# A third addition of u and of its square, and one of e, ahead of the sums of chunks 1 to 4, with another order of the work

## The chip, the cores and the metric

The kernel runs on one core of a Trainium2 chip. The metric is the device time of one execution in microseconds. The core has five engines, each of which works through its own list of instructions in order: PE (matmuls; a weight load goes ahead of each), DVE and ACT (elementwise work), POOL (elementwise work, and the issue of most loads) and SP (which here only issues transfers).

## What is computed

Linear attention without a softmax, normalized by head, is followed by a feed-forward layer with SoLU (h times the softmax of h) and a layer norm inside. In the reference, for 8 batches of 8 heads with 576 rows of 64, and a feed-forward of 512 to 1024 to 512 on all 4608 rows:

```python
kv = np.einsum('bhsd,bhse->bhde', k, v)
out = np.einsum('bhsd,bhde->bhse', q, kv)
rms = np.sqrt(np.mean(out * out, axis=-1, keepdims=True) + 1e-06)
x = out / rms * g_norm            # heads side by side: 4608 x 512
h = x @ w_in
e = np.exp(h - h_max)
solu = h * (e / (np.sum(e, axis=-1, keepdims=True) + 1e-09))
ln = (solu - mu) / np.sqrt(var + 1e-06) * g_ln
return ln @ w_out
```

## The kernel before

The rows go in nine **chunks** of 512: chunks 0 to 7 take eight of every nine rows of one batch each, and chunk 8 takes the ninth row of all batches. The names below are those of the kernel's table of work; the first number is the chunk or batch.

- `kv_mm` multiplies k by v of a batch on PE, and `kv` casts the products out of PSUM. Batches 0 and 1 come in two halves of four heads (second number 0 and 1); `qT_mm` and `qT` turn q. `o_mm` gives o, `sq` squares it on ACT, `oa` adds the two halves of the squares, and `s_mm` sums them by head. `ex` (chunk 0: one instruction; later `ln` and `ex`) gives the reciprocal root, and `x` (L489, DVE) scales o by it. `table` loads ACT's second function table between the two kinds of root.
- `h` (L532) multiplies x by w_in: eight blocks per chunk, four matmuls each, in two parts for chunks 0 to 2. `exp` (L539, ACT) makes e, and `u` (L543, DVE) is h times e. `usq` (L233 on ACT or L235 on POOL) is u squared, and `es` (L551, POOL) adds e of two neighbouring blocks, so that eight become four.
- The layer norm needs three sums over all 1024 columns, of u, u squared and e. **`sums`** (L594) makes them on PE, as matmuls with a small selecting matrix, four for each block of 512 that is left. Before that, `ua`, `usqa` and `esa` (all L575, in `fold`, on DVE) add the upper half of the blocks to the lower half: `FOLDS` says how often for u and u squared (eight blocks become four, two, one) and `E_FOLDS` for e (four become two). `turn` (L601), `stats` and `rstd` make the factor of each row of it.
- `w_mean` and `w_center` prepare w_out once, with the mean and the weight of the layer norm in it. `out` (L651) multiplies u by it, four blocks of rows per chunk, eight matmuls each; the last block of chunk 8 is done in two halves of columns (L659). `ob` (L239 on ACT, L241 on DVE) scales by `rstd`, and `store` sends it off.
- `warm` (L300) is matmuls on zeros whose result nobody reads; `WARM` holds how many there are at each of seven places. `ident` (POOL) makes the identity for `qT_mm`, and `wide` loads the second half of k and v of batch 0 as float32 through SP, which `k.0.1` and `v.0.1` cast.

Nothing here is scheduled by a compiler. `ORDER` is a table of all the pieces of work, written out by hand or by a program, and `Plan.emit` records them one by one: each engine's list is what the table gives it in this order, with the engine behind a colon where it isn't the usual one. `ROOMS` holds a digit for each tile that says which of its slots it takes; for the tiles in PSUM that is one of eight banks, and a piece that takes a bank waits until the work on what stood there is done. So an instruction waits for its data, for its room, and for all that stands ahead of it on its engine. Beyond that, `Plan.run` makes each POOL instruction wait for the additions that DVE was given ahead of it:

```python
if engine == "pool":
    self.after(ins, self.adds)
    self.adds.clear()
if name[0] in ("ua", "usqa", "esa", "oa") and engine == "dve":
    self.adds.append(ins)
```

Of the kernel before, what the change touches and what calls it, by code (L numbers as in the profile page):

```python
# [25 lines left out]
kv.1.0.0.0 kv.1.0.1.1 kv.1.0.1.0 qT_mm.1.0 ex.0.0 q.2.0 qT.1.0:act x.0.0.0 x.0.0.1 warm.5 o_mm.1.0 sq.1.0.0 warm.6
h.0.6.0 h.0.3.0 k.2.0 sq.1.0.1 x.0.1.0 table h.0.0.0 oa.1.0 x.0.1.1 s_mm.1.0 h.0.2.0 h.0.7.0 h.0.2.1 ln.1.0 v.2.0
ex.1.0 h.0.6.1 x.1.0.1 exp.0.6 q.3.0 h.0.3.1 exp.0.2 x.1.0.0 h.0.7.1 h.0.1.0 exp.0.7 u.0.6 v.3.0 qT_mm.1.1 h.0.0.1
exp.0.3 h.0.1.1 u.0.2 usq.0.6 h.1.2.0 exp.0.0 qT.1.1 kv_mm.1.1.1 exp.0.1 kv_mm.1.1.0 k.3.0 kv.1.1.0.1 h.0.4.0 h.0.4.1
u.0.1 kv.1.1.2.1:act kv.1.1.0.0:act es.0.0 kv.1.1.1.0:act kv.1.1.2.0:act kv.1.1.1.1 u.0.3 o_mm.1.1 exp.0.4 h.0.5.0  # L30
u.0.7 sq.1.1.0 es.0.3 h.0.5.1 u.0.4 sq.1.1.1 h.1.0.0 w_mean.0 usq.0.1:act oa.1.1 u.0.0 exp.0.5 s_mm.1.1 ln.1.1 ex.1.1
u.0.5 es.0.2 w_mean.1 w_mean.2 w_mean.3 w_mean.4 w_mean.5 w_mean.6 usq.0.5:act x.1.1.1 usq.0.2 usq.0.7:act w_mean.7
x.1.1.0 usq.0.0 q.4.0 usq.0.4:act w_center.5 h.1.3.0 qT_mm.2.1 h.1.7.0 w_center.1 h.1.4.0 h.1.7.1 qT.2.1:act q.5.0
w_center.4 h.1.0.1 v.4.0 w_center.0 exp.1.7 qT_mm.2.0 exp.1.0 w_center.3 h.1.1.0 h.1.1.1 k.4.0 qT.2.0:act w_center.2
h.1.2.1 es.0.1 u.1.7 h.1.3.1 exp.1.1 h.1.4.1 u.1.0 exp.1.3 out.0.2.0 es.1.0 usq.0.3 u.1.1 exp.1.2 out.0.2.1 kv_mm.2.0
w_center.7 exp.1.4 h.1.5.0 w_center.6 kv.2.1.0:act kv.2.0.0:act h.1.5.1 kv.2.0.2:act kv.2.1.1 kv.2.0.1:act es.1.1
u.1.4 out.0.2.2 kv.2.1.2:act exp.1.5 o_mm.2.0 u.1.3 o_mm.2.1 sq.2.0.1 out.0.2.3 usq.1.1 u.1.2 qT_mm.3.0 sq.2.0.0 u.1.5
out.0.0.0 sq.2.1.1 oa.2.0 out.0.0.1 sq.2.1.0 qT.3.0 s_mm.2.0 usq.1.5 out.0.0.2 ln.2.0 qT_mm.3.1 oa.2.1:pool ex.2.0
h.1.6.0 qT.3.1 out.0.0.3 usq.1.2:act x.2.0.0 x.2.0.1 h.1.6.1 s_mm.2.1 exp.1.6 sums.0 usq.1.7 ln.2.1 u.1.6 ex.2.1
kv_mm.3.0 es.1.2 turn.0 stats.0 out.0.3.0 kv.3.1.0:act x.2.1.0 x.2.1.1 usq.1.0:act out.0.3.1 usq.1.4 usq.1.3 h.2.6.0  # L40
out.0.3.2 rstd.0 h.2.0.0 ob.0.0:act usq.1.6 kv.3.0.1 ob.0.2 h.2.6.1 kv.3.1.2:act kv.3.0.0:act kv.3.1.1:act out.0.3.3
usqa.1.0 kv.3.0.2:act h.2.4.0 exp.2.6 h.2.5.0 ob.0.3:act ua.1.0 o_mm.3.0 h.2.1.0 store.0.3 sq.3.0.0 h.2.0.1 sq.3.0.1
u.2.6 h.2.1.1 store.0.0 exp.2.0 h.2.5.1 usqa.1.1 out.0.1.0 exp.2.1 oa.3.0 h.2.4.1 ua.1.1 exp.2.5 qT.4 s_mm.3.0
out.0.1.1 u.2.0 ln.3.0 es.1.3 out.0.1.2 u.2.5 h.2.7.0 ex.3.0 h.2.7.1 u.2.1 exp.2.4 es.2.0 h.2.3.0 x.3.0.1 exp.2.7
o_mm.3.1 sq.3.1.0 x.3.0.0 usq.2.6 out.0.1.3 sq.3.1.1 h.2.2.0 h.2.3.1 u.2.7 qT.5 ob.0.1:act h.2.2.1 oa.3.1 sums.1
exp.2.3 u.2.4 es.2.3 kv_mm.4.0 exp.2.2 u.2.3 store.0.1 usq.2.5:act s_mm.3.1 turn.1 es.2.2 out.1.3.0 kv.4.1.0
kv.4.0.1:act ln.3.1 u.2.2 store.0.2 out.1.3.1 kv.4.0.0 usq.2.7 ex.3.1 stats.1 out.1.2.0 kv.4.0.2:act kv.4.1.1 kv.4.1.2
rstd.1 x.3.1.1 usq.2.0 o_mm.4.0 o_mm.4.1 ob.1.3 sq.4.0.1 out.1.0.0 usq.2.4 x.3.1.0 sq.4.0.0 store.1.3 out.1.2.1
sq.4.1.0 oa.4.0 ua.2.0 sq.4.1.1 s_mm.4.0 out.1.0.1 ln.4.0 oa.4.1 h.3.2.0 ex.4.0 ob.1.0 v.5.0 s_mm.4.1 x.4.0.0 h.3.7.0
k.5.0 ln.4.1 x.4.0.1 exp.3.2 es.2.1 h.3.3.0 ex.4.1 u.3.2 h.3.6.0 exp.3.3 ua.2.1 exp.3.7 h.3.5.0 x.4.1.0 u.3.3 v.6.0  # L50
exp.3.6 x.4.1.1 h.3.1.0 exp.3.5 q.6.0 usq.2.2:act h.3.4.0 usq.3.3 ob.1.2:act usq.2.1:act usq.2.3:act exp.3.4 es.3.1
u.3.7 u.3.5 store.1.2 h.4.6.0 u.3.6 k.6.0 u.3.4 h.4.7.0 exp.3.1 out.1.1.0 out.1.1.1 exp.4.7 usq.3.2:act h.3.0.0
usqa.2.0 usqa.2.1 exp.4.6 ob.1.1:act u.4.7 kv_mm.5.0 usq.3.5 exp.3.0 u.3.1 sums.2 kv.5.0.1:act es.3.3 h.4.5.0
usq.4.7:act u.4.6 kv.5.0.0:act kv.5.1.2:act h.4.4.0 q.7.0 kv.5.0.2 kv.5.1.1:act u.3.0 kv.5.1.0:act exp.4.5 o_mm.5.1
es.3.0 turn.2 o_mm.5.0 sq.5.1.0 out.2.3.0 stats.2 u.4.5 sq.5.1.1 out.2.3.1 exp.4.4 oa.5.1 ua.3.0 rstd.2 s_mm.5.1
out.2.0.0 ln.5.1 u.4.4 sq.5.0.0 out.2.0.1 sq.5.0.1 ua.3.1 h.4.0.0 ob.2.3:act oa.5.0 ob.2.0 ex.5.1 s_mm.5.0 es.4.2
store.2.3 h.4.2.0 ln.5.0 x.5.1.0 h.4.3.0 store.1.1 usq.3.6 exp.4.2 x.5.1.1 ex.5.0 usq.3.4:act kv_mm.6.0 u.4.2 usq.3.0
qT.6 out.2.1.0 out.2.2.0 kv.6.1.0 kv.6.0.0 es.4.3 kv.6.1.2 x.5.0.0 out.2.2.1 usq.3.7:act qT.7 x.5.0.1 exp.4.3
usq.3.1:act h.4.1.0 es.3.2 kv.6.1.1:act u.4.3 usq.4.5:act kv.6.0.1 ob.2.2:act store.1.0 usqa.3.0 h.5.3.0 exp.4.1
kv.6.0.2:act h.5.6.0 store.2.0 exp.5.3 exp.4.0 usqa.3.1 u.4.1 h.5.7.0 es.4.0 es.4.1 usq.4.6:act u.4.0 out.2.1.1  # L60
exp.5.6 u.5.3 exp.5.7 o_mm.6.0 ob.2.1 o_mm.6.1 sq.6.0.0 sums.3 u.5.6 store.2.1 out.3.0.0 sq.6.0.1 u.5.7 usq.4.2:act
oa.6.0 out.3.0.1 sq.6.1.1 ua.4.0 sq.6.1.0 s_mm.6.0 out.3.3.0 ln.6.0 oa.6.1 turn.3 out.3.3.1 ex.6.0 v.7.0 stats.3
q_last.3 s_mm.6.1 x.6.0.0 h.5.0.0 ln.6.1 k.7.0 x.6.0.1 h.5.2.0 ex.6.1 q_last.1 exp.5.0 x.6.1.0 h.5.5.0 q_last.7
exp.5.2 u.5.0 h.5.4.0 rstd.3 es.5.1 x.6.1.1 usq.4.4:act out.3.1.0 ob.3.0 exp.5.4 es.5.3 h.6.6.0 usq.4.3:act ob.3.3
usq.4.0:act u.5.4 h.6.3.0 exp.5.5 ua.4.1 h.5.1.0 usq.4.1:act u.5.5 q_last.0 exp.6.6 out.3.1.1 u.5.2 q_last.4
# [670 lines left out]
```

## Time and profile before

| what | value |
|---|---|
| time, median of 3 runs | 177.52 us (177.48 to 177.98) |
| span of the profiled execution | 175.8 us |
| granted clock of TensorE, mean | 1.000 |
| PE / DVE / ACT / POOL busy | 164.2 / 145.5 / 152.1 / 99.8 us |
| matmuls of h and of out in the profile | 280 of 68.0 us, 266 of 65.2 us |
| HBM read, written | 32.51 MB, 9.44 MB |

The span runs from the first to the last instruction in one profiled execution. The times of the runs hold what lies around the span as well; the profiled execution's own time is not given apart from it. Matmuls overlap, so a mean of 379 ns says how long one is under way, not how far apart two start. In the rows, "out<-in" names the tiles written and read, a figure in square brackets or behind the last bar is the idle time of the engine just before, and the name behind an arrow is what ended it.

### The profile page before, as it was taken

The page shows a single profiled execution, that of the slowest core. Times are in us where ns is not written, and L with a number is a line of the kernel's source. Part 1 is how long each engine was busy: PE and PEld are TensorE (multiplying, and loading weights), DVE is VectorE, ACT ScalarE, POOL GpSimd, SP SyncE. Part 2 cuts the span into 40 slices and gives each one's busy share as a digit, 9 for nine tenths or more (in the row PEclk, how much of TensorE's full clock was granted, in tenths as well). Part 3 has the DMA queues.
Part 4 walks back from the last instruction along what each step waited for, and adds up shares of the span by engine and source line. Part 5 has one row for each costly group of instructions (what it writes and reads, how often), then busy time and mean ns, then how long its engine had stood idle before and what let it go on. Part 6 is the DMA issues. An engine that isn't in the chain of part 4 may idle for free.

```text
span 175.8 us, 4843 instructions
## 1 busy us (share of the span) xinstructions
PE 164.2 (93%) x1913; PEld 80.3 (46%) x1938; DVE 145.5 (83%) x317; ACT 152.1 (86%) x273; POOL 99.8 (57%) x108
## 2 busy tenths in 40 slices
PE   7767998798999999999999999999999999999992
PEld 2344344454564354445454444445464444444451
DVE  2015769899899999989999999979997999998732
ACT  2549899998999998999999999999999989999450
POOL 8744359899790794877294567593191257335000
PEclk9999999999999999999999999999999999999999
DMA  5999999999999995899989639983994055024874
GB/s 179 218 203 214 206 275 373 209 208 208 208 210 210 218 210 129 127 206 235 205 183 259 150 52 193 156 73 93 195 206 105 5 118 126 2 60 93 196 213 159
DMA packets 34623, 30.27 MB, mean 172 GB/s; under 512 B 16288, under 2 KB 28328, under 8 KB 34600
## 3 DMA queue, kind: packets, MB, share of 16 engines
...
HBM read 32.51 MB, written 9.44 MB: 239 GB/s over the span
## 4 chain that ended last, share of the span: by engine, by line
PE 75%; DVE 10%; ACT 5%; DMA 5%; issue 2%; POOL 1%; POOLq 0%; DVEq 0%; ACTq 0%
PE h_ps L532 31%; PE out_ps L651 30%; DMA k_sb<-in_k_dram 5%; PE kv_ps L375 4%; PE o_ps L448 3%; DVE u_sb L543 3%; PE sum_ps L594 3%; PE s_ps L465 3%; DVE x_sb L489 2%; DVE w_out_sb L638 2%; ACT osq_sb L233 2%; DVE osq_sb L460 1%; PE out_ps L659 1%; ACT e_sb L539 1%; ACT kvd L229 1%
## 5 line engine op out<-in xcount | busy, mean ns | idle before, releaser
L532 PE MATMUL h_ps<-x_sb,w_in_sb 128*128 128x512 bf16 x280 | 68.0, 379 | 0.5
L651 PE MATMUL out_ps<-w_out_sb,u_sb 128*128 128x512 bf16 x266 | 65.2, 379 | 0.7 <-issue 0.3
L551 POOL TENSOR_TENSOR es_sb<-e_sb 128x512 bf16<-128x512 f32 x36 | 45.4, 1279 | 33.5 <-ACT e_sb L539 13.0
L539 ACT ACTIVATE e_sb<-h_ps,zero_t 128x512 f32<-128x512 f32 x72 | 46.2, 690 | 2.3 <-PE h_ps L532 1.7
L543 DVE TENSOR_TENSOR u_sb<-h_ps,e_sb 128x512 bf16<-128x512 f32 x72 | 46.6, 684 | 1.3 <-ACT e_sb L539 1.0
L532 PEld LDWEIGHTS <-w_in_sb 128*128 128x128 bf16 x288 | 27.3, 98 | 32.5 <-issue 1.3
L651 PEld LDWEIGHTS <-u_sb 128*128 128x128 bf16 x280 | 26.4, 98 | 31.6 <-issue 1.0
L233 ACT ACTIVATE usq_sb<-u_sb,zero_t 128x512 bf16<-128x512 bf16 x49 | 33.6, 718 | 0.0
L489 DVE SCALAR_TENSOR_TENSOR x_sb<-o_ps,g_sb,rst_sb 128x256 bf16<-128x256 f32 x72 | 30.2, 478 | 3.1 <-ACT rst_sb L476 2.5
L235 POOL TENSOR_TENSOR usq_sb<-u_sb 128x512 bf16<-128x512 bf16 x23 | 23.6, 1043 | 7.9 <-DVE osq_sb L460 5.6
L233 ACT ACTIVATE osq_sb<-o_ps,zero_t 128x512 bf16<-128x512 f32 x36 | 22.8, 689 | 3.5 <-PE o_ps L448 3.4
L239 ACT ACTIVATE ob_sb<-out_ps,rstd 128x512 f32<-128x512 f32 x22 | 14.8, 684 | 4.0 <-PE out_ps L651 3.8
L575 DVE TENSOR_TENSOR usq_sb<-usq_sb 128x2048 bf16<-128x2048 bf16 (+2 forms) x20 | 17.0, 848 | 0.6 <-ACT usq_sb L233 0.4
L229 DVE CAST kvd<-kv_ps 64x128 bf16<-64x128 f32 (+3 forms) x26 | 6.4, 256 | 11.2 <-ACT kvd L229 6.5
L241 DVE TENSOR_SCALAR ob_sb<-out_ps,rstd 128x512 f32<-128x512 f32 (+1 forms) x15 | 10.6, 711 | 4.1 <-PE out_ps L659 2.2
L322 POOL DMA_DIRECT2D v_sb<-in_v_dram x9 | 6.8, 757 | 10.1 <-DVE sum_ps L601 2.8
L472 ACT ACTIVATE lss_sb<-s_ps,eps_t 128x512 f32<-128x512 f32 x16 | 11.1, 695 | 1.0 <-PE s_ps L465 0.7
L476 ACT ACTIVATE rst_sb<-lss_sb,zero_t 128x512 f32<-128x512 f32 x16 | 11.5, 722 | 0.4
L375 PE MATMUL kv_ps<-v_sb,k_sb 64*64 64x64 bf16 x576 | 8.0, 194 | 2.8 <-DMA k_sb<-in_k_dram 1.3
L300 PE MATMUL warm_ps<-zeros 128*128 128x512 bf16 x25 | 8.8, 481 | 1.4 <-DVE zeros L255 1.2
L229 ACT CAST kvd<-kv_ps 64x128 bf16<-64x128 f32 (+3 forms) x34 | 8.2, 243 | 2.2 <-PE kv_ps L375 1.5
L375 PEld LDWEIGHTS <-k_sb 64*64 64x64 bf16 x576 | 6.8, 107 | 6.8 <-DMA k_sb<-in_k_dram 2.6
...
## 6 DMA issues: line engine op xcount, KB each, us to landing
...
```

The lines of the kernel that those rows point to most:

```text
L229: nc.scalar.copy(dst, src) if engine == "act" else on[engine].tensor_copy(dst, src)
L233: nc.scalar.activation(out=dst, in_=src, func=AF.Square, bias=zero_t[:, :])
L235: on[engine].tensor_tensor(out=dst, in0=src, in1=src, op=MUL)
L239: nc.scalar.activation(out=dst, in_=src, func=AF.Copy, scale=by)
L375: nc.tensor.matmul(t[64 * y:64 * y + 64, :], T["k", b][rows, n, i, :], T["v", b][rows, n, i, :], start=(i == 0 and (b < 2 or m == 0)), sto ...
L489: nc.vector.scalar_tensor_tensor(out=t[:, 2 * hf + dh, z], in0=T["o", c, hf, z][:, dh], scalar=g_rep[dh], in1=T["rst", c, hf][:, z], op0=M ...
L532: nc.tensor.matmul(bank(("h", c, f), [128, 512])[:, :], w_in_sb[:, dt, f * 128:(f + 1) * 128], T["x", c][:, dt].rearrange("p a b c -> p (a ...
L539: nc.scalar.activation(out=t[:, f % 2, :], in_=T["h", c, f][:, :], func=AF.Exp, bias=zero_t[:, :])
L543: nc.vector.tensor_tensor(out=t[:, f, :], in0=T["h", c, f][:, :], in1=T["e", c, f // 2][:, f % 2, :], op=MUL)
L551: on[engine].tensor_tensor(out=t[:, n, :], in0=e[:, 0, :], in1=e[:, 1, :], op=ADD)
L575: nc.vector.tensor_tensor(out=to[:, 0:n, :], in0=src[:, 0:n, :], in1=src[:, n:2 * n, :], op=ADD)
L651: nc.tensor.matmul(bank(("out", c, m), [128, d_model])[:, :], T["u", c][:, f, m * 128:(m + 1) * 128], w_out_sb[:, f, :], start=(f == 0), s ...
```

## The change

Chunks 1 to 4 get what chunks 5 to 8 had: a third addition of u and of u squared, which leaves one block of each instead of two, and one addition of the e blocks, which leaves two instead of four. So `sums` of these chunks has 4 x (1 + 1 + 2) = 16 matmuls instead of 32. The whole table is another one too: order, engines and rooms differ from the first piece on, and the numbers of matmuls on zeros. The loads through POOL come in the same succession, and the stores nearly so. Counted over the table, these change engines or number:

| pieces | before | after |
|---|---|---|
| additions `ua`, `usqa`, `esa` on DVE | 20, 20, 4 | 24, 24, 8 |
| `oa` on DVE, POOL | 15, 1 | 11, 5 |
| `ob` on DVE (of them halves), ACT (halves) | 15 (2), 22 | 11 (0), 26 (2) |
| `kv` on DVE, ACT | 26, 34 | 21, 39 |
| `usq` on POOL, ACT | 23, 49 | 27, 45 |
| cast of the wide k | ACT | DVE |
| matmuls on zeros | 27 | 42 |

```diff
@@ ORDER, the first and the last lines @@
-wide.v ident wide.k g_rows q.0.1 v.0.0 k.0.0 q.0.0 v.0.1:act v.1.0 k.1.0 q.1.0 w_in.0 k.0.1:act w_in.1 warm.0
-kv_mm.0.1.0 qT_mm.0.1 kv.0.1.0.0:act kv.0.1.1.0 kv_mm.0.1.1 q.1.1 qT.0.1:act kv.0.1.2.1 kv.0.1.2.0 kv.0.1.1.1
...
-out.8.1.1 out.8.3.0 rstd.8 ob.8.2:act ob.8.0 store.8.2:act store.8.0 ob.8.1:act store.8.1:act ob.8.3.0 store.8.3.0
-out.8.3.1 ob.8.3.1 store.8.3.1:act
+wide.v v.0.1:act wide.k g_rows q.0.1 v.0.0 k.0.0 q.0.0 v.1.0 k.1.0 q.1.0 w_in.0 k.0.1 ident warm.0 qT_mm.0.1 w_in.1
+q.1.1 warm.1 kv_mm.0.0.0 kv.0.0.2.0:act kv.0.0.1.0:act kv_mm.0.0.1 v.1.1 k.1.1 w_out.0 w_out.1 kv.0.0.0.1:act
...
+store.8.2 store.8.0:act store.8.1:act ob.8.3.0:act ob.8.3.1:act store.8.3.0 store.8.3.1:act
@@ ROOMS @@
...
@@ WARM @@
-14 3 1 3 1 4 1
+21 11 5 1 1 2 1
@@ tile_transnormer_attn__then__act_solu_kernel @@
-    FOLDS = (0, 2, 2, 2, 2, 3, 3, 3, 3)
-    E_FOLDS = (0, 0, 0, 0, 0, 1, 1, 1, 1)
+    FOLDS = (0, 3, 3, 3, 3, 3, 3, 3, 3)
+    E_FOLDS = (0, 1, 1, 1, 1, 1, 1, 1, 1)
```

Three places, by what stands there on an engine. First ACT in the head, from the squares of o of batch 0 to the table load. Before (`o_ps_303` and `_305` are half 1 of batch 0, `_347` and `_349` half 0, `_458` and `_460` batch 1; `rst_sb` are the reciprocal roots):

```order
L233 ACTIVATE osq_sb_322<-o_ps_303,zero_t_81 128x2x256
L233 ACTIVATE osq_sb_371<-o_ps_347,zero_t_81 128x2x256
L233 ACTIVATE osq_sb_371<-o_ps_349,zero_t_81 128x2x256
L482 ACTIVATE rst_sb_403<-s_ps_373,eps_t_79 128x512
L229 CAST kvd_1_0_0_1_110<-kv_ps_382 128x64
L482 ACTIVATE rst_sb_442<-s_ps_425,eps_t_79 128x512
L229 COPY qT_sb_446<-qt_ps_433 128x1024
L233 ACTIVATE osq_sb_476<-o_ps_458,zero_t_81 128x2x256
L233 ACTIVATE osq_sb_476<-o_ps_460,zero_t_81 128x2x256
L494 ACT_TABLE_LOAD
```

After (here `o_ps_347` and `_349` are half 0, `_422` and `_424` half 1, `_478` and `_480` batch 1):

```order
L233 ACTIVATE osq_sb_391<-o_ps_347,zero_t_81 128x2x256
L233 ACTIVATE osq_sb_391<-o_ps_349,zero_t_81 128x2x256
L482 ACTIVATE rst_sb_397<-s_ps_394,eps_t_79 128x512
L233 ACTIVATE osq_sb_451<-o_ps_422,zero_t_81 128x2x256
L233 ACTIVATE osq_sb_451<-o_ps_424,zero_t_81 128x2x256
L229 CAST kvd_1_0_2_0_113<-kv_ps_371 64x64
L229 CAST kvd_1_0_0_0_109<-kv_ps_371 128x64
L229 CAST kvd_1_0_1_0_111<-kv_ps_371 64x64
L482 ACTIVATE rst_sb_472<-s_ps_467,eps_t_79 128x512
L233 ACTIVATE osq_sb_496<-o_ps_480,zero_t_81 128x2x256
L233 ACTIVATE osq_sb_496<-o_ps_478,zero_t_81 128x2x256
L494 ACT_TABLE_LOAD
```

Half 0 now comes first, with its root; the squares of half 1, three casts for batch 1 and the root of half 1 stand between it and batch 1's squares. The turning copy has gone to DVE.

Second, DVE between chunk 1 and chunk 2. Before, from the scaling of a block of chunk 0 (`ob_sb`) through the additions of chunk 1 (`usq_sb_897`, `ua_sb_1178`) among the first u of chunk 2 (`u_sb_1208`):

```order
L241 TENSOR_SCALAR ob_sb_1157<-out_ps_752,rstd_1148 128x512
L575 TENSOR_TENSOR usq_sb_897<-usq_sb_897 128x2048
L575 TENSOR_TENSOR ua_sb_1178<-u_sb_742 128x2048
L543 TENSOR_TENSOR u_sb_1208<-h_ps_1141,e_sb_1171 128x512
L575 TENSOR_TENSOR usq_sb_897<-usq_sb_897 128x1024
L460 TENSOR_TENSOR osq_sb_1203<-osq_sb_1203 128x512
L575 TENSOR_TENSOR ua_sb_1178<-ua_sb_1178 128x1024
L543 TENSOR_TENSOR u_sb_1208<-h_ps_1150,e_sb_1214 128x512
L543 TENSOR_TENSOR u_sb_1208<-h_ps_1173,e_sb_1227 128x512
```

After, from the last product x of chunk 2 through the additions of chunk 1 (`usq_sb_784`, `ua_sb_1034`, `es_sb_776`) to the first u of chunk 2 (`u_sb_1230`):

```order
L489 SCALAR_TENSOR_TENSOR x_sb_1080<-o_ps_985,g_sb_73,rst_sb_1085 128x256 x2
L229 CAST kvd_3_1_1_131<-kv_ps_1097 64x128
L229 COPY qT_sb_1092<-qt_ps_1175 128x1024
L575 TENSOR_TENSOR usq_sb_784<-usq_sb_784 128x2048
L575 TENSOR_TENSOR usq_sb_784<-usq_sb_784 128x1024
L575 TENSOR_TENSOR ua_sb_1034<-ua_sb_1034 128x512
L575 TENSOR_TENSOR es_sb_776<-es_sb_776 128x1024
L575 TENSOR_TENSOR usq_sb_784<-usq_sb_784 128x512
L543 TENSOR_TENSOR u_sb_1230<-h_ps_1216,e_sb_1228 128x512
L543 TENSOR_TENSOR u_sb_1230<-h_ps_1235,e_sb_1228 128x512
```

The additions of chunk 1 that are left at this place, five of its seven, now stand together ahead of all u of chunk 2; two of u (with 2048 and 1024 elements) stand further up, ahead of that chunk's x.

Third, the end of ACT's list. Before (`out_ps_3197` and `_3272` are blocks of chunk 8):

```order
L615 ACTIVATE lv_3290<-vare_3264,zero_t_81 128x4
L617 ACTIVATE rstd_3292<-lv_3290,zero_t_81 128x4
L239 ACTIVATE ob_sb_3294<-out_ps_3197,rstd_3292 128x512
L675 DMA out_0_dram<-ob_sb_3294 128x512
L239 ACTIVATE ob_sb_3300<-out_ps_3272,rstd_3292 128x512
L675 DMA out_0_dram<-ob_sb_3300 128x512
L675 DMA out_0_dram<-ob_sb_3303 128x256
```

After (`out_ps_3158` and `_3255` are the two halves of the last block):

```order
L615 ACTIVATE lv_3247<-vare_3245,zero_t_81 128x4
L617 ACTIVATE rstd_3249<-lv_3247,zero_t_81 128x4
L239 ACTIVATE ob_sb_3270<-out_ps_3230,rstd_3249 128x512
L675 DMA out_0_dram<-ob_sb_3264 128x512
L675 DMA out_0_dram<-ob_sb_3270 128x512
L239 ACTIVATE ob_sb_3275<-out_ps_3158,rstd_3249 128x256
L239 ACTIVATE ob_sb_3275<-out_ps_3255,rstd_3249 128x256
L675 DMA out_0_dram<-ob_sb_3275 128x256
```

The two last halves, which DVE scaled, now stand on ACT behind the issue of two stores.

More of the change, by code (lines that the diff above doesn't have):

```diff
@@ L26 @@
[L26 to L65, printed above, removed]
@@ new lines @@
+u.8.1 out.6.0.0 out.7.2.0 h.8.2.0 out.7.0.0 out.6.0.1 out.6.1.0 out.6.1.1 u.8.0 u.7.7 h.8.3.0 out.7.0.1 out.6.2.0
+usq.8.0:act ob.6.3 out.6.2.1 out.7.3.0 store.6.3 usq.7.7:act usq.7.0:act usq.7.6:act usq.8.4:act usq.8.7:act es.8.3
+es.8.0 es.7.3 ua.7.0 esa.7.0 exp.8.2 exp.8.3 ua.7.1 ob.6.1:act ob.6.0:act usqa.7.0 usqa.7.1 ua.7.2 usqa.7.2 u.8.3
+sums.7 out.7.3.1 es.8.1 u.8.2 out.8.2.0 store.6.0 usq.8.6:act turn.7 stats.7 es.8.2 esa.8.0 usq.8.1:act out.7.2.1
+out.7.1.0 out.8.3.0 out.7.1.1 ua.8.0 ob.6.2:act out.8.0.0 out.8.0.1 usq.8.2:act rstd.7 ob.7.3:act ob.7.0:act
```

94 lines of the change are left out of this document (65 added, 29 removed).

## The prediction

> **What bounds the kernel now.** I read the page first: the busy times, and the span in 40 equal slices.
>
> ```profile
> span 175.8 us, 4843 instructions
> PE 164.2 (93%) x1913; PEld 80.3 (46%) x1938; DVE 145.5 (83%) x317; ACT 152.1 (86%) x273; POOL 99.8 (57%) x108
> PE   7767998798999999999999999999999999999992
> DVE  2015769899899999989999999979997999998732
> ```
>
> The PE row is full from about the tenth slice to the last but one. There the program is a queue of matmuls, and its time is the start of that queue, plus its matmuls, plus its stops, plus the tail behind it. Next the table of windows, which gives busy us per stretch (columns: span, length, PE, PEld, DVE, ACT, POOL, clock, DMA share, GB/s).
>
> ```profile
> 0.00:5.00 5.00, 3.81 (x9) 1.34 (x10) 0.90 (x14) 1.35 (x2) 4.29 (x13) 1.00 0.59 207
> 5.00:10.00 5.00, 3.57 (x52) 1.84 (x51) 0.80 (x4) 3.52 (x5) 2.92 (x5) 1.00 1.14 191
> 35.00:40.00 5.00, 4.84 (x28) 2.27 (x27) 5.00 (x9) 4.66 (x8) 4.82 (x6) 1.00 1.22 208
> 40.00:45.00 5.00, 4.48 (x123) 2.68 (x126) 4.94 (x10) 4.22 (x11) 3.69 (x5) 1.00 1.22 208
> 45.00:65.00 20.00, 19.82 (x363) 10.15 (x366) 18.81 (x45) 19.23 (x36) 14.22 (x13) 1.00 1.21 207
> 65.00:100.00 35.00, 34.63 (x438) 16.52 (x443) 33.39 (x66) 33.98 (x65) 22.03 (x22) 1.00 0.97 191
> ```
>
> Three stages follow. Before 20 us the input transfers and a chain of short steps set the pace. From there to 45 us DVE has no free time and PE still stops. From 45 us PE is the bound, with little room behind it: DVE has 1.19 us free in 45 to 65 and 1.61 in 65 to 100, ACT 0.77 and 1.02. POOL alone has room.
>
> **The change part by part: the sums.** In the chain of waits, which keeps what PE was held by, sums of a chunk with two additions and of one with three stand side by side:
>
> ```profile
> 119.44 0.56 PE sum_ps L594 x32
> 130.04 0.34 PE sum_ps L594 x16
> ```
>
> Four chunks go from 32 matmuls to 16: 4 x 0.22 = 0.88 us off PE, nearly all where PE is the bound. **Term: -0.9.**
>
> **The additions, and what leaves DVE for them.** From the groups that keep shapes apart:
>
> ```profile
> L575 DVE TENSOR_TENSOR usq_sb<-usq_sb 128x512 bf16<-128x512 bf16 x4 | 1.7, 423 | 0.0
> L575 DVE TENSOR_TENSOR ua_sb<-ua_sb 128x512 bf16<-128x512 bf16 x4 | 1.7, 419 | 0.0
> L575 DVE TENSOR_TENSOR es_sb<-es_sb 128x1024 bf16<-128x1024 bf16 x4 | 2.7, 685 | 0.0
> L460 DVE TENSOR_TENSOR osq_sb<-osq_sb 128x512 bf16<-128x512 bf16 x15 | 6.7, 445 | 1.0 <-ACT osq_sb L233 0.6
> L241 DVE TENSOR_SCALAR ob_sb<-out_ps,rstd 128x512 f32<-128x512 f32 x13 | 9.6, 747 | 1.9 <-ACT rstd L617 1.0 <-PE out_ps L651 0.9
> L229 DVE CAST kvd<-kv_ps 64x128 bf16<-64x128 f32 x10 | 2.9, 289 | 1.5 <-PE kv_ps L375 0.9 <-ACT kvd L229 0.3
> L460 POOL TENSOR_TENSOR osq_sb<-osq_sb 128x512 bf16<-128x512 bf16 x1 | 1.1, 1150 | 0.0
> L235 POOL TENSOR_TENSOR usq_sb<-u_sb 128x512 bf16<-128x512 bf16 x23 | 23.6, 1043 | 7.9 <-DVE osq_sb L460 5.6 <-DVE usq_sb L575 2.2
> L239 ACT ACTIVATE ob_sb<-out_ps,rstd 128x512 f32<-128x512 f32 x22 | 14.8, 684 | 4.0 <-PE out_ps L651 3.8
> L233 ACT ACTIVATE usq_sb<-u_sb,zero_t 128x512 bf16<-128x512 bf16 x49 | 33.6, 718 | 0.0
> ```
>
> Added to DVE: 4 x (0.419 + 0.423 + 0.685) = 6.1 us. Off DVE over the whole program: four additions of o squared (1.8), two full scalings and the last two halves (2.5), five casts (about 1.3); the net is near zero. ACT gets those casts and scalings and loses four squares of u (2.9); POOL gets four squares and four additions of o squared, 4 x (1.043 + 1.150) = 8.8 us, of the 76 it has free. The relief is not where the load is, though. All 6.1 us fall on chunks 1 to 4, that is on 45 to about 110 us; of the relief there, DVE scales five blocks of chunks 0 to 3 where it scaled eight (2.2), adds net two fewer o squares (0.9) and casts two fewer (0.6). That leaves +2.4 us, against the 2.8 us that DVE has free between 45 and 100. So the cost for PE lies between 0 (every free moment gets used) and 2.4 (none does). The order shows the worst place: behind the last product x of chunk 2, five additions of chunk 1 now stand in one row, about 3.4 us by their rows, ahead of the first u of chunk 2, and PE's later products of chunk 2 need the banks that u frees. Before, two additions stood ahead of it. I take 1.0, below the middle, since the rest is spread out. **Term: +1.0.**
>
> A rule weighs against this part. The additions have two operands in SBUF; one of them met a POOL instruction:
>
> ```profile
> 30.23 0.79 DVE L460 TENSOR_TENSOR osq_sb<-osq_sb 128x512 bf16<-128x512 bf16 x1
> 28.21 2.52 POOL L551 TENSOR_TENSOR es_sb<-e_sb 128x512 bf16<-128x512 f32 x2
> ```
>
> It took 0.79 us instead of 0.445 and ended 0.3 us after POOL did, at 30.73. The Trainium skill, "SBUF — State Buffer", section "Who interferes with whom", says that such a DVE instruction and a POOL instruction that reads SBUF exclude each other, and the later one waits for the whole of the earlier. The trace agrees at this place. By that rule alone, with each of twelve additions waiting half of a 1.28 us POOL addition, the sum would be 7.7 us more; by the rows, it is next to nothing, since hardly any addition of the program is longer than its group's mean, the kernel making each POOL instruction wait for the additions ahead of it.
>
> **The head.** The order of the two halves of batch 0 is turned round. Rows of the timeline (start, length):
>
> ```profile
> 14.08 0.62 PE L448 MATMUL o_ps<-qT_sb,kvd 64*32 64x256 bf16 x16 [0.29 <-ACT kvd L229]
> 15.77 0.76 PE L375 MATMUL kv_ps<-v_sb,k_sb 64*64 64x64 bf16 x36
> 19.11 0.43 PE L448 MATMUL o_ps<-qT_sb,kvd 64*32 64x256 bf16 x16 [0.24 <-DVE x_sb L489]
> 19.84 1.47 PE L532 MATMUL h_ps<-x_sb,w_in_sb 128*128 128x512 bf16 x6
> 14.28 1.84 ACT L233 ACTIVATE osq_sb<-o_ps,zero_t 128x512 bf16<-128x512 f32 x3
> 17.10 0.69 ACT L482 ACTIVATE rst_sb<-s_ps,eps_t 128x512 f32<-128x512 f32 x1 [0.30 <-PE kv_ps L375]
> 20.90 1.28 ACT L494 ACT_TABLE_LOAD   x1
> 23.67 3.00 ACT L539 ACTIVATE e_sb<-h_ps,zero_t 128x512 f32<-128x512 f32 x5
> ```
>
> At 14.08 PE multiplies half 0; half 1 had been done before it, in the wait for a transfer. Now half 0 comes first, at about the same 14.1, since its inputs land as before, and half 1 stands in PE's queue behind both products k·v of batch 1. I follow it with those lengths. Squares of half 0 done 16.0; PE meanwhile five warm matmuls and the first k·v of batch 1; sums, the second k·v, and half 1's product at 17.4. The root of half 0 ends at 17.7 (17.79 before). Squares of half 1 18.1 to 19.4 and three casts to 19.9, which batch 1's product needs: 20.0 where it was 19.11. DVE puts two casts and a 0.69 us copy between the two x products of half 0. Two warm matmuls more, and the first h starts at 20.9 instead of 19.84. On ACT the root of half 1 (20.1) and batch 1's squares end at 22.0, the table is in at 23.3, and the first exponential starts at 24.8, not 23.67: **1.1 us late**, on the chain that feeds DVE's full stretch. Nothing hides it: DVE has nothing to do earlier.
>
> Against it stands an earlier start of the loads. The identity is now made behind the first w_in load:
>
> ```profile
> 1.63 0.89 POOL L322 DMA_DIRECT2D q_sb<-in_q_dram  x1
> 0.74 0.20 POOL masks.py:197 MEMSET ident<- 128x128 bf16 x1 [0.29 <-POOLq L720]
> ```
>
> The first load goes out 0.89 us sooner. But the windows above show the engines' share at 0.59 in the first 5 us, while the two wide loads of SP run, and at 1.14 after: the early loads mostly share with those. Between 0 and -0.9 I take -0.1, nearest to what the share allows. The cast of the wide k moves to DVE, for which there is no row; between 0.7 and 1.15 us by casts of like size, in a stretch in which DVE is idle (0.80 busy of 5), so it costs nothing. More warm matmuls fill PE's waits, at no cost up to the ones counted. **Term: +1.0.**
>
> **The tail.** ACT now also scales the last two halves, behind two store issues:
>
> ```profile
> 169.64 0.38 ACTq L675 DMA_DIRECT2D out_dram<-ob_sb  x1
> 172.57 0.48 DVE L241 TENSOR_SCALAR ob_sb<-out_ps,rstd 128x256 f32<-128x256 f32 x1 [0.39 <-PE out_ps L659]
> ```
>
> Sums of chunk 8 now have four blocks of matmuls behind them (3.45 us) instead of six. The last reciprocal root is ready 2.1 us after those sums begin; then ACT scales a block (0.68), issues twice (0.76), and scales two halves, each between 0.34 (half of 0.684) and 0.68, say 0.45. The last half ends about 0.9 us behind the last matmul, where it was 0.5. Between 0 and +0.8, **term: +0.4.**
>
> **The sum**: -0.9 + 1.0 + 1.0 + 0.4 = +1.5 on a span of 175.8, so 177.3. The median of the runs shown, 177.52, stands 1.7 above that span, and with the same around it the time is **179.0**.
>
> **The rivals.** *Faster: the waits of the second stage go.* Three stops of PE were:
>
> ```profile
> 31.08 0.38 PE L465 MATMUL s_ps<-osq_sb,head_mean 128*128 128x512 bf16 x1 [0.71 <-DVE osq_sb L460]
> 34.08 0.62 PE L427 MATMUL qt_ps<-ident,q_sb 128*128 128x128 bf16 x8 [0.57 <-DMA q_sb<-in_q_dram]
> 40.40 0.77 PE L375 MATMUL kv_ps<-v_sb,k_sb 64*64 64x64 bf16 x72 [0.51 <-DVE u_sb L543]
> ```
>
> All h of chunk 1 now stand ahead of chunk 2's q, and half of two output blocks ahead of its k·v, so PE need not stop for these transfers. If 1.8 us of stops go and DVE keeps up, the sum is -0.9 + 1.0 - 1.8 + 0.4 = -1.3: 176.2. It decides at DVE: 5.00 of 5 in 35 to 40 and 4.94 in 40 to 45, and the third stop already waits for DVE. DVE, starting 1.1 us late with the same products, u and centring to do, can't be ahead; that speaks against it.
>
> *Level: the lateness is caught up and DVE finds its gaps.* Then -0.9 and +0.4 remain: 177.0.
>
> *Slower still: DVE's free time isn't usable.* The 2.4 us in place of the 1.0: 180.4, and port waits by the rows' 0.35 each could take it to 181.
>
> *The change does less than it says*: the order on each engine shows the twelve additions and the 16-matmul sums in place, so no.
>
> **How the numbers follow.** 0.3% of the time, 0.53 us, is about what a measurement can tell from no change. Forecast, 178.0 to 180.2: 0.45; faster rival: 0.20; level: 0.15; slower still: 0.20. Level and the lowest end of the forecast lie within 0.53: 0.17; faster 0.20; slower 0.63. The range from 176.6 to 181.2 leaves out most of the faster rival alone.
>
> **What would show it.** Head: first h at 20.5 to 21 and first exponential at 24.4 to 24.9; if they stand at 19.8 and 23.7, that term is wrong. Additions: DVE at 98% of its time between 45 and 110 us, and PE stopping for u of chunk 2 behind the five additions; with PE unbroken there, the level case holds. Sums: 0.34 us each for chunks 1 to 4. Tail: the last scaling on ACT, starting after the second issue. Wrong altogether if PE reaches chunk 2's k·v with h of chunk 1 complete before 42 us.

## The result, and the profile after

The changed kernel took 187.86 us (median of 4 runs, 185.59 to 189.88), the kernel before 177.51 (177.48 to 177.98): a ratio of 1.0543, with an interval of 1.0498 to 1.0588. The ratio here, and each one below, leaves out runs more than 1.5% above the fastest of their kernel (here 189.88), so it need not be the quotient of the medians. The forecast was 179.0 with a range from 176.6 to 181.2. The profiled execution is the fastest of the four: 185.59 us, a span of 183.8, 8.0 more than before. The runs of before lie within 0.5 us, those of after spread over 4.3, and about 2.3 us of the median stand in no profile.

The page of after, in the lines that were shown of before:

```profile
span 183.8 us, 4803 instructions
PE 169.1 (92%) x1889; PEld 80.9 (44%) x1889; DVE 149.6 (81%) x317; ACT 151.5 (82%) x277; POOL 111.1 (60%) x116
PE   7998998998988989999999998978998999999990
DVE  1226778898989988999898999969978799798950
```

PE's row has lost its unbroken stretch of nines: eights and a seven stand in it up to about the thirtieth slice. DVE and ACT are busy for a smaller share than before; POOL has 11 us more. The windows (columns as before):

```profile
40.00:45.00 5.00, 4.62 (x199) 3.14 (x196) 4.09 (x8) 4.70 (x11) 5.00 (x6) 1.00 1.22 209
45.00:65.00 20.00, 18.37 (x255) 8.79 (x251) 18.47 (x40) 18.42 (x35) 11.61 (x12) 1.00 0.94 171
65.00:100.00 35.00, 33.38 (x410) 15.47 (x396) 32.60 (x70) 32.68 (x63) 21.74 (x21) 1.00 0.95 173
100.00:125.00 25.00, 22.03 (x227) 10.10 (x224) 22.44 (x41) 23.79 (x44) 21.38 (x20) 1.00 0.85 133
```

The last of these windows in the kernel before:

```profile
100.00:125.00 25.00, 24.84 (x241) 11.69 (x243) 23.58 (x49) 24.28 (x46) 14.65 (x16) 1.00 0.86 122
```

Between 45 and 125 us PE is idle for 6.2 us, where it was idle for 0.7 (0.18 and 0.37 in the two windows that the prediction shows, and 0.16 here). From 125 to 145 us it is idle for 0.96, where it was 0.21. DVE and ACT are less busy between 45 and 125 us than before, not more: three engines wait for one another in turn, none is the bound. POOL is busy 21.38 of 25 us in the last window, where it was 14.65.

What PE waited for, 45 to 130 us (columns: who waits, for whom, us, times, longest; four more rows have 0.2 us each). The same view of before has no row at all:

```profile
PE o_ps L448 <- ACT kvd L229: 2.4, 2, 1.4
PE sum_ps L594 <- DVE u_sb L543: 1.9, 1, 1.9
PE h_ps L532 <- DVE x_sb L489: 0.6, 1, 0.6
```

Casts of k·v ahead of an attention, a product u ahead of the sums of chunk 4, an x ahead of an h: each a different partner. The one in the middle shows how such a stop is made. The timeline of after: ACT, then PE's products k·v of chunk 7 (their last part), DVE, and PE again (start, length, in brackets the idle time ahead and what ended it):

```profile
121.74 0.80 ACT L229 CAST kvd<-kv_ps 128x128 bf16<-128x128 f32 x3
...
119.81 0.38 PE L375 MATMUL kv_ps<-v_sb,k_sb 64*64 64x64 bf16 x24
...
119.81 1.32 DVE L575 TENSOR_TENSOR usq_sb<-usq_sb 128x2048 bf16<-128x2048 bf16 x1
122.57 0.29 DVE L229 CAST kvd<-kv_ps 128x128 bf16<-128x128 f32 x1 [1.45 <-ACT kvd L229]
122.78 1.31 DVE L575 TENSOR_TENSOR usq_sb<-usq_sb 128x1024 bf16<-128x1024 bf16 x2
124.01 1.88 DVE L543 TENSOR_TENSOR u_sb<-h_ps,e_sb 128x512 bf16<-128x512 f32 x3
...
124.75 0.24 PE L594 MATMUL sum_ps<-ua_sb,stat_sel 128*32 128x128 bf16 x4 [1.86 <-DVE u_sb L543]
```

DVE stands idle for 1.45 us ahead of a cast whose bank PE had filled over 2 us before (the second row), until ACT's cast of the same bank is done. Both only read that bank; in chunks 2 to 7 of both traces two casts of one bank on two engines never overlap, they go in the order of the list (why, no run shows). Behind DVE's cast stand two additions, behind them the u that frees a bank, and PE waits for all of it.

And the place where DVE meets POOL. DVE, then POOL:

```profile
108.53 2.09 DVE L575 TENSOR_TENSOR ua_sb<-ua_sb 128x1024 bf16<-128x1024 bf16 x2
110.54 3.22 DVE L489 SCALAR_TENSOR_TENSOR x_sb<-o_ps,g_sb,rst_sb 128x256 bf16<-128x256 f32 x8
...
102.64 1.04 POOL L235 TENSOR_TENSOR usq_sb<-u_sb 128x512 bf16<-128x512 bf16 x1 [3.89 <-DVE ua_sb L575]
103.96 1.27 POOL L551 TENSOR_TENSOR es_sb<-e_sb 128x512 bf16<-128x512 f32 x1 [0.29 <-PE o_ps L448]
105.19 2.24 POOL L460 TENSOR_TENSOR osq_sb<-osq_sb 128x512 bf16<-128x512 bf16 x1
```

Two additions of chunk 4, 0.68 and 0.42 us elsewhere, take 2.09 while POOL is running; x of chunk 6 and its h wait behind them. POOL is still busy there, having waited 3.89 us for the additions of chunk 3 before; from 104 to 118 us it has no pause. Over 45 to 126 us POOL's listed waits for DVE's additions are 24.0 us, where they were 14.6.

### The profile page after: what moved, and what is told of

It reads as the page before. It is cut to its first block, busy times and chain, and to the rows that moved or that the text cites. A ratio compares the mean times of both kernels' runs of the same rounds, so it can differ in the third digit from the quotient of the medians.

```text
span 183.8 us, 4803 instructions
## 1 busy us (share of the span) xinstructions
PE 169.1 (92%) x1889; PEld 80.9 (44%) x1889; DVE 149.6 (81%) x317; ACT 151.5 (82%) x277; POOL 111.1 (60%) x116
## 4 chain that ended last, share of the span: by engine, by line
PE 53%; ACT 17%; DVE 13%; issue 5%; POOL 4%; DMA 4%; SPq 2%; ACTq 0%; POOLq 0%
PE h_ps L532 25%; PE out_ps L651 17%; DMA out_dram<-ob_sb 4%; DVE x_sb L489 4%; ACT usq_sb L233 4%; ACT e_sb L539 3%; ACT kvd L229 3%; ACT osq_sb L233 3%; ACT ob_sb L239 3%; PE kv_ps L375 2%; DVE ua_sb L575 2%; SPq L679 2%; PE warm_ps L300 2%; PE sum_ps L594 2%; PE o_ps L448 2%
## 5 line engine op out<-in xcount | busy, mean ns | idle before, releaser
L651 PE MATMUL out_ps<-w_out_sb,u_sb 128*128 128x512 bf16 x280 | 67.1, 379 | 0.3
L235 POOL TENSOR_TENSOR usq_sb<-u_sb 128x512 bf16<-128x512 bf16 x27 | 28.0, 1051 | 15.1 <-DVE ua_sb L575 9.0
L233 ACT ACTIVATE usq_sb<-u_sb,zero_t 128x512 bf16<-128x512 bf16 x45 | 30.7, 717 | 0.1
L239 ACT ACTIVATE ob_sb<-out_ps,rstd 128x512 f32<-128x512 f32 (+1 forms) x26 | 17.1, 669 | 4.2 <-DMA out_dram<-ob_sb 3.2
L575 DVE TENSOR_TENSOR usq_sb<-usq_sb 128x2048 bf16<-128x2048 bf16 (+2 forms) x24 | 19.1, 795 | 0.9 <-ACT usq_sb L233 0.7
L300 PE MATMUL warm_ps<-zeros 128*128 128x512 bf16 x42 | 12.3, 437 | 1.4 <-DVE zero_t L259 1.2
L229 DVE CAST kvd<-kv_ps 64x64 bf16<-64x64 f32 (+3 forms) x21 | 5.3, 255 | 8.1 <-ACT kvd L229 5.1
L322 POOL DMA_DIRECT2D q_sb<-in_q_dram x10 | 7.7, 770 | 6.1 <-DVE ua_sb L575 4.0
L460 POOL TENSOR_TENSOR osq_sb<-osq_sb 128x512 bf16<-128x512 bf16 x5 | 6.9, 1372 | 7.1 <-DVE usq_sb L575 4.1
L448 PE MATMUL o_ps<-qT_sb,kvd 64*32 64x256 bf16 (+1 forms) x384 | 7.4, 246 | 4.1 <-ACT kvd L229 2.4
```

The costliest lines, as they stand in the source:

```text
L229: nc.scalar.copy(dst, src) if engine == "act" else on[engine].tensor_copy(dst, src)
L233: nc.scalar.activation(out=dst, in_=src, func=AF.Square, bias=zero_t[:, :])
L235: on[engine].tensor_tensor(out=dst, in0=src, in1=src, op=MUL)
L239: nc.scalar.activation(out=dst, in_=src, func=AF.Copy, scale=by)
L300: nc.tensor.matmul(t[:, :], zeros[:, 0:128], zeros[:, :], start=True, stop=True)
L575: nc.vector.tensor_tensor(out=to[:, 0:n, :], in0=src[:, 0:n, :], in1=src[:, n:2 * n, :], op=ADD)
```

## The experiments

Three theories were set against each other. A: the twelve additions on DVE make the stops. S: the new succession makes them, additions or not. E: the new engines of casts, squares and scalings do. All times are medians in us, each ratio is to the kernel before in the same session (its medians: 177.50 to 177.70).

**e1: the changed kernel without the additions.**

```diff
-    FOLDS = (0, 3, 3, 3, 3, 3, 3, 3, 3)
-    E_FOLDS = (0, 1, 1, 1, 1, 1, 1, 1, 1)
+    FOLDS = (0, 2, 2, 2, 2, 3, 3, 3, 3)
+    E_FOLDS = (0, 0, 0, 0, 0, 1, 1, 1, 1)
-ua.1.2 usqa.1.2 esa.1.0 ua.2.2 usqa.2.2 esa.2.0 ua.3.2 usqa.3.2 esa.3.0 ua.4.2 usqa.4.2 esa.4.0
```

> The changed kernel without its twelve new additions (third additions of u and its square and the one of e in chunks 1 to 4; sums of 32 matmuls again); order, engines and zero-products as changed. Theory A (the additions on VectorE stop PE between 50 and 125 us, where 7.4 us of PE's time went): the stops go, sums cost 0.9 more, so 187.9 - 7.4 + 0.9 = 181, between 179 and 183. Theory S (the new succession stops PE by itself, additions or not): 186 to 190. Between 183 and 186: a share each.

188.12, ratio 1.0571 (1.0515 to 1.0626): the same as with them. PE's waits stand where they stood:

```profile
PE sum_ps L594 <- DVE u_sb L543: 2.2, 1, 2.2
PE o_ps L448 <- ACT kvd L229: 2.2, 2, 1.4
```

A falls as the cause by itself.

**e2 and e8: the kernel before with the additions,** first with that of e right ahead of the sums (shown for chunk 1, and with the same constants as the change), then earlier.

```diff
 ua.1.1
+ua.1.2
 ...
 usqa.1.1
+usqa.1.2
 ...
+esa.1.0
 sums.1
```

> The kernel before with the twelve additions put into its own order (each third one right behind the second, that of e ahead of the sums; sums of 16 matmuls in chunks 1 to 4). Theory A: 177.5 + 7.4 - 0.9 = 184, between 182 and 186. Theory S: within 1.5 of the kernel before, 176 to 179.

> The kernel before with the twelve additions, but the one of e no longer right ahead of the sums: earlier on VectorE, behind the end of its data (before the last product of chunk 2, the first additions of squares of chunks 2 and 3, behind the additions of u of chunk 4). PE waited 4.1 us for that addition where it stood last. If the place made the cost: 178.5 to 180.5, so that the additions by themselves cost 1 to 3. If VectorE has no room for 6.1 us anywhere: 182 to 185 again.

e2: 183.54, ratio 1.0349 (1.0295 to 1.0404). e8: 181.76, ratio 1.0229 (1.0195 to 1.0262). In e2 one wait carries most of it:

```profile
PE sum_ps L595 <- DVE es_sb L576: 4.1, 4, 1.6
```

In e8 it is gone, and what is left is some ten waits for DVE of at most 0.5 us. In the old order 6.1 us of additions thus cost 4.2 us, or 5.1 with the 0.9 that the shorter sums give: DVE has hardly any room. Taken out of the new order they give nothing clear of its spread, with the 0.9 that the longer sums cost allowed for. A cost that is paid when added and not refunded when removed belongs to no single instruction; the kernel is held by whichever wait ends last.

**e3: the changed kernel with the old engines** for 79 pieces (casts, squares, additions of squares of o, scalings), places kept.

```diff
-kv.7.0.0:act
+kv.7.0.0
-oa.4.0:pool
+oa.4.0
 ...
```

> The changed kernel with the engines of the kernel before for every cast of k.v, square of u, addition of squares of o and scaling of the output that the change had given to another (79 pieces); their places in the order stay. Theory E (the casts given to ACT and the squares given to POOL stop PE): 179 to 183. Theories A and S: 185 to 191, since additions and order stay.

210.33, ratio 1.1836 (1.1811 to 1.1861), 22 us slower still. E falls in this form: the order and the engines belong together.

**e4: the tail.**

```diff
-ob.8.3.0:act ob.8.3.1:act
+ob.8.3.0 ob.8.3.1
```

> The changed kernel with the last two half blocks scaled on VectorE as before; all else as changed. The time behind the last matmul falls from 4.5 us to 3.5 to 4.0, and the whole by 0.4 to 1.0, to 187; if the end waits for stores and not for ACT, it stays at 4.5 and 188.

189.41, ratio 1.065 (1.0613 to 1.0687). The edit lies behind the last matmuls, yet the stops at 103 to 125 us are larger in its profile than in that of after (2.7 us ahead of the sums of chunk 4, where it was 1.9). The changed order, built and run again, thus comes out about 1.5 us apart (187.86 and 189.41); differences of that size between its variants are read below from their stops, not from their times. The tail got 0.2 us shorter, not 0.4 to 1.0: the last matmuls begin at 182.66 and the span ends at 187.7, against 178.55 and 183.8.

**e5: three casts to the other engine. e6: the additions of squares of o to DVE. e7: both.**

```diff
-kv.3.1.1 ... kv.4.1.2:act ... kv.7.1.0
+kv.3.1.1:act ... kv.4.1.2 ... kv.7.1.0:act
```

```diff
-oa.3.0:pool ... oa.4.0:pool ... oa.6.0:pool ... oa.7.0:pool ... oa.8.1:pool
+oa.3.0 ... oa.4.0 ... oa.6.0 ... oa.7.0 ... oa.8.1
```

> The changed kernel with three casts of k.v given to the other engine: kv.3.1.1 and kv.7.1.0 from VectorE to ACT, kv.4.1.2 from ACT to VectorE; nothing else. Theory K: VectorE and ACT take the casts of one bank in the order of the list, so one late engine holds the other, and these three casts make the stops of 1.5 us ahead of the attention of chunk 3, 1.1 of chunk 4 and 1.9 ahead of the sums of chunk 4. K: those three stops fall under 0.5 each, and the time by 3 to 4.5, to 183 to 185. Rival L (both engines are simply behind, the wait moves to the next word): stops of like size a few us later, 186.5 to 189.

> The changed kernel with the five additions of squares of o that POOL does (chunks 3, 4, 6, 7, 8) on VectorE, as ten others are. Theory P (POOL, which takes 1.2 to 2.2 us for one where VectorE takes 0.42, makes the norms of chunks 4 and 6 late): stops at 78 and 108 to 111 us fall by some 1.5 together, 186 to 186.5. Rival: VectorE is as late by 2.1 us of work, 187.5 to 189.

> Both edits: the three casts and the five additions of squares. Theories K and P both right: 181.5 to 183.5. If each stop comes back elsewhere: 186 to 189.

e5: 185.77, ratio 1.0462 (1.0404 to 1.0519). Its longest waits:

```profile
PE h_ps L532 <- DVE x_sb L489: 1.5, 2, 1.3
PE o_ps L448 <- DVE u_sb L543: 0.8, 2, 0.6
PE sum_ps L594 <- DVE ua_sb L575: 0.6, 1, 0.6
PE o_ps L448 <- ACT kvd L229: 0.5, 1, 0.5
PE sum_ps L594 <- DVE u_sb L543: 0.3, 1, 0.3
```

The stops for casts fell from 2.4 to 0.5 us, that of the sums of chunk 4 from 1.9 to 0.3: K holds for them. But 0.6 us more is now lost at other attentions, 0.6 ahead of the sums of chunk 3 and 0.9 at x of chunk 6. The time fell by 1.4 (by the ratios) to 2.1 (by the medians), not 3 to 4.5, and the intervals of the two ratios overlap. By the stops 3.5 us were mended and 2.1 came back elsewhere, as L said. e6: 193.51, ratio 1.085 (1.0777 to 1.0922); e7: 190.49, ratio 1.072 (1.0676 to 1.0764), both slower than any range expected of them. P falls. In e6 the two additions of chunk 4, which took 2.09 us in after, took 3.38:

```profile
113.30 3.38 DVE L575 TENSOR_TENSOR ua_sb<-ua_sb 128x1024 bf16<-128x1024 bf16 x2
```

From this came theory C: an addition that meets a running POOL instruction waits, and all behind it. Nominal, from here on, is the time of an addition that meets none: 0.42 us for 512 elements, 0.685 for 1024, 1.22 for 2048.

**e9: these two additions behind x. e10: POOL's words into its pause, from their places further down. e12: both, all three on top of e5.**

```diff
-ua.4.1 s_mm.6.1 ln.6.1 ua.4.2 ... x.6.1.1 x.6.1.0
+s_mm.6.1 ln.6.1 ... x.6.1.1 x.6.1.0 ua.4.1 ua.4.2
```

```diff
 usq.3.7
+usq.4.4 v.7.0 q_last.3 k.7.0 q_last.1 q_last.7 q_last.0 q_last.4 q_last.6
 usqa.3.0
```

> The three casts of e5 kept; besides, the second and third addition of u of chunk 4 go behind the four products of x of chunk 6 on VectorE (they stood ahead of them and took 1.60 and 1.14 us in e5, where nominal is 0.68 and 0.42, while POOL ran its backlog). Theory C (an addition that meets a running POOL instruction waits for it, and x and the next products behind it): the stop of 1.7 us ahead of h.5.4.0 falls under 0.5, and the time from 185.8 to 184 to 185. Rival L (it moves to the next word): 185.5 to 187.

> The three casts of e5 kept; besides, one square (usq.4.4) and eight loads (v and k of batch 7 and six of the last quarter of q) go ahead of the additions of chunk 3 in the list, into the 4.4 us in which POOL waits for those additions at 98 us. POOL's backlog at 104 to 126 us shrinks by 7 us. Theory C: the additions of chunk 4 meet POOL less (3.8 us over nominal in e5, then under 2), and the time falls to 183.5 to 185. If POOL's lateness plays no part: 185.3 to 187.

> The changed kernel with all mends: the casts of e5, the additions of e9, the POOL words of e10. If the stops are separate: 182 to 184. If the succession as a whole keeps giving them back: 185 to 187.

e9: 191.28, ratio 1.0776 (1.0734 to 1.0819). x was no longer held, but the additions met POOL at a worse moment. DVE, POOL, PE:

```profile
112.63 5.57 DVE L575 TENSOR_TENSOR ua_sb<-ua_sb 128x1024 bf16<-128x1024 bf16 x2
...
111.96 1.07 POOL L235 TENSOR_TENSOR usq_sb<-u_sb 128x512 bf16<-128x512 bf16 x1
112.97 1.29 POOL L551 TENSOR_TENSOR es_sb<-e_sb 128x512 bf16<-128x512 f32 x1
114.20 1.05 POOL L235 TENSOR_TENSOR usq_sb<-u_sb 128x512 bf16<-128x512 bf16 x1
115.19 1.27 POOL L551 TENSOR_TENSOR es_sb<-e_sb 128x512 bf16<-128x512 f32 x1
...
118.85 1.44 PE L532 MATMUL h_ps<-x_sb,w_in_sb 128*128 128x512 bf16 x3 [4.85 <-DVE u_sb L543]
```

These four POOL instructions kept their usual lengths, one behind the other; DVE's 1.1 us became 5.57, and PE stood for 4.85. e10: 194.37, ratio 1.0956 (1.0897 to 1.1016), and e12: 191.79, ratio 1.0815 (1.0769 to 1.0861), were misplaced: the load of v waited until chunk 6's attention had begun, with POOL's addition of squares of o behind eight loads. PE waited for that, in e12:

```profile
PE s_ps L465 <- POOL osq_sb L460: 5.1, 1, 5.1
```

Their times say nothing on C.

**e11 and e16: the rule taken away,** in the kernel before and in the changed one.

```diff
         if engine == "pool":
-            self.after(ins, self.adds)
             self.adds.clear()
```

> The kernel before without the rule that a POOL instruction waits for the additions on VectorE listed ahead of it; data waits stay, order stays. Theory C: additions and POOL's instructions now meet freely, additions take 4 us or more over nominal in sum (0.7 with the rule), and the time is 179 to 183. If they don't disturb each other: POOL runs ahead, 177 to 178.

> The changed kernel without the rule that POOL waits for the additions listed ahead of it (the kernel before lost 8.7 us by that, its additions 12 us over nominal). Theory C: additions 12 us or more over nominal here too, 192 to 200. If POOL's waits by that rule cost the changed kernel as much as meetings do: 185 to 190.

e11: 186.38, ratio 1.05 (1.047 to 1.053). e16: 201.58, ratio 1.1385 (1.1312 to 1.1457). Same instructions, same order, fewer waits, and 8.7 and 13.7 us slower. Groups of e11 (their counterparts of before: 445, and 423 in the prediction):

```profile
L459 DVE TENSOR_TENSOR osq_sb<-osq_sb 128x512 bf16<-128x512 bf16 x15 | 10.0, 667 | 1.2 <-ACT osq_sb L232 1.0
L574 DVE TENSOR_TENSOR usq_sb<-usq_sb 128x512 bf16<-128x512 bf16 x4 | 3.6, 896 | 0.0
```

All of DVE's additions together, summed over such groups, take 43.4 us before and 55.1 in e11, and 50.1 in after and 69.3 in e16. Taken one by one, the additions beside which no POOL instruction ran (56 in before, 50 in after, 30 in e11, 31 in e16) are within 0.1 us of nominal in sum in each kernel. Those beside an elementwise POOL instruction (2, 12, 23, 32) are longer by 0.5, 2.7, 12.2 and 22.0 us. C is shown, and so is what the rule buys. In after, twelve more at their nominal lengths and four of o less would make 47.7, so its 50.1 hold 2.4 us more of meetings than before.

**e13: POOL's late words listed behind the additions they met (with the casts of e5). e15: the same without the twelve additions. e18: e15 with the loads and `es.5.1` left where they stood.**

```diff
-usq.4.0 ... es.4.1 ... q_last.3 ... usq.5.6 es.5.0 ... usq.4.2 es.4.0 ... ua.4.2
+ua.4.2 usq.4.0 es.4.1 q_last.3 usq.5.6 es.5.0 usq.4.2 es.4.0
```

```diff
-q_last.1 q_last.7 q_last.0 q_last.4 ... q_last.6 es.5.1 ... usqa.4.2
+usqa.4.2 q_last.1 q_last.7 q_last.0 q_last.4 q_last.6 es.5.1
```

> The three casts of e5 kept; besides, POOL's words that ran late into the additions of chunk 4 are listed behind them: three squares, three additions of e and one load behind ua.4.2, five loads and one addition of e behind usqa.4.2, so that the rule holds POOL back and not the port VectorE. Theory C: ua.4.1, ua.4.2 and usqa.4.2, 2.7 us over nominal in e5, fall to under 0.5, the stop of 1.7 us at h.5.4.0 to under 0.5, and the time from 185.8 to 183 to 185. Rival L (POOL, held back, is late for the next): 185.5 to 190.

> e13 without the twelve new additions (sums of 32 matmuls in chunks 1 to 4). If they cost VectorE nothing in this succession, as taking them out of the changed kernel alone did: equal to e13 or 0.9 slower. If they cost once the stops are mended: 1 to 4 faster than e13.

> The changed kernel with the three casts of e5, the seven POOL words of chunk 4 behind ua.4.2 as in e13 (the five loads and es.5.1 where they stood), and without the twelve additions. If casts, meetings and additions are what holds the changed kernel back up to 125 us, and the stop of 3.9 us ahead of the attention of chunk 7 in e13 came from the loads that were moved: 181.5 to 184. If the succession gives each mend back: 186 to 188.

e13: 188.33, ratio 1.0626 (1.0575 to 1.0676). At the mended place C holds: the pair of additions takes its nominal time, and no wait of PE for x is left in its list from 100 to 140 us. The time is outside C's 183 to 185, and all additions together still take 50.0 us: others met POOL.

```profile
108.44 1.14 DVE L575 TENSOR_TENSOR ua_sb<-ua_sb 128x1024 bf16<-128x1024 bf16 x2
```

But POOL, held back, came late to the next norm, as L said:

```profile
PE s_ps L465 <- POOL osq_sb L460: 3.5, 1, 3.5
```

e15: 186.88, ratio 1.0531 (1.0475 to 1.0587), 1.5 below e13, too little to read by itself. e18: 183.63, ratio 1.0335 (1.0319 to 1.0351). Its longest wait of PE between 45 and 135 us is 0.5. The three casts, the meetings mended and the additions are thus together worth 4.2 of the 10.3 us (3.7 by the ratios). How it divides among them no run shows; the casts alone gave 1.4 to 2.1. Nor are the meetings gone: the additions of e18 take 43.8 us, 2.2 more than the same ones would by before (41.6), nearly the 2.4 of after.

**e14 and e17: the kernel before with `ident` behind the first load of w_in,** nothing else; e17 is e14 timed again.

```diff
-wide.v ident wide.k ... w_in.0 k.0.1:act
+wide.v wide.k ... w_in.0 ident k.0.1:act
```

> The kernel before with the making of ident moved behind the first load of w_in, as in the changed kernel; nothing else. The first loads go out 0.89 us sooner. If the head of the kernel follows the loads one to one: 176.6 to 177.2; if they share the engines of the transfers: within 0.3 of the kernel before.

> The same kernel as e14, timed again with more rounds, since its interval of ratios (0.9969 to 1.0002) still held no change: if the 0.9 us of its profiled span is real, a ratio of 0.994 to 0.998; if it was the scatter of one profile, 0.999 to 1.001.

e14: 177.25, ratio 0.9986 (0.9969 to 1.0002); e17: 177.19, ratio 0.9973 (0.9957 to 0.9989). The first exponentials, e14 and e17:

```profile
22.85 2.42 ACT L539 ACTIVATE e_sb<-h_ps,zero_t 128x512 f32<-128x512 f32 x4
23.10 2.42 ACT L539 ACTIVATE e_sb<-h_ps,zero_t 128x512 f32<-128x512 f32 x4
```

0.6 to 0.8 us sooner than the 23.67 of before; at the end 0.25 to 0.5 of it is left. This word alone makes the one version that is faster than both kernels, by 0.1 to 0.3%; only the interval of e17 leaves out no change.

## Why the prediction was wrong

**Sums, -0.9: right where the chain shows one.** Chunk 1's in the chain of waits of after, where 0.34 was named:

```profile
63.04 0.37 PE sum_ps L594 x16
```

**Head, +1.0: wrong, about 0.** The first h starts at 19.86 (19.84 before; 20.9 was named), and the first exponential of after stands where it stood (23.67 before), not at 24.8:

```profile
23.68 1.84 ACT L539 ACTIVATE e_sb<-h_ps,zero_t 128x512 f32<-128x512 f32 x3
```

The step that failed is the -0.1 for the earlier loads, taken from a range of 0 to -0.9. e14 and e17 measure 0.6 to 0.8 for it; the rest of the new head must then cost about as much, since the two cancel. That is inferred, not tried by itself.

**Additions, +1.0 (0 to 2.4): wrong. It was the whole price of the stretch from 45 us on, and there most of the time went.** Between 45 and 125 us PE is idle 5.5 us more than before, and DVE is not the engine at its limit: from 45 to 110 us it is busy for 60.3 of 65 us, 93%, where 98% was named. The cost is not that of the additions alone either, since e1 without them loses as much. The named sign, PE stopping for u of chunk 2 behind the five additions, did not come; PE stopped for a cast of chunk 3:

```profile
55.76 0.43 PE L448 MATMUL o_ps<-qT_sb,kvd 64*32 64x256 bf16 x16 [1.43 <-ACT kvd L229]
```

As an estimate, DVE's own work was not mis-sized: in e8 6.1 us of it without any relief cost 5.1, and 3.7 of relief off that leaves 1.4, near the 1.0. The term failed because it stopped there, in two steps. "POOL gets ... 8.8 us, of the 76 it has free" took free time for room. Of the 25.6 us that the waits of POOL list between 45 and 126 us of before, 14.6 are for DVE's additions, and in after 24.0; with more work behind such waits POOL was late, and met the next additions. And the rule of the ports was read and set aside. By the Trainium skill, "SBUF — State Buffer", section "Who interferes with whom", the two exclude each other, from which the prediction estimated 7.7 us more. It took next to nothing, since hardly any addition of before is longer than its group. That was true of a list in which POOL is on time. e11 shows 11.7 us of it in the very kernel that showed next to none. The casts, too, were priced as work (0.6 us of relief), not as places at which two engines wait for each other.

**Tail, +0.4 (0 to 0.8): mechanism in part, size 0.9.** The last matmuls begin at 178.55 and take 1.04, so the span goes on for 4.2 us behind them, where it was 3.3 (170.62 and 1.91 before). The scaling is on ACT behind its store issues as said, but its wait ended with a store that frees a buffer, and the last half ends 1.4 us behind the last matmul, where 0.9 was named:

```profile
180.20 0.84 ACT L239 ACTIVATE ob_sb<-out_ps,rstd 128x256 f32<-128x256 f32 x2 [1.57 <-DMA out_dram<-ob_sb]
```

In e4 DVE ends the halves 0.7 us behind the last matmul and the span still gets only 0.2 us shorter, so the scaling is not what holds most of the 0.9; the rest stays open.

**The rivals.** "Slower still: DVE's free time isn't usable", with port waits on top, named a mechanism that the runs show (C) and ended at 181, 7 us short: it let each addition wait 0.35 us, and let no wait make another. The limit for "wrong altogether" was nearly met: PE reached chunk 2's k·v at 42.0 us with h of chunk 1 complete. The faster rival was right up to there, in that its three stops are gone from after, and fell behind it.

**What stays open.** e18 is still 6.1 us above the kernel before, with no wait of PE over 0.5 us in the list up to 135 us, so more than half of the change's cost has no shown cause. About 0.9 is the tail. In the profile of e18 PE is idle for 3.75 us between 45 and 125 us (0.70 in before) and for 1.48 between 125 and 145 (0.21), in small stops; no run isolates them.
